# Which queue issues the stores and the first loads of a fused attention and adapter kernel

## The chip, the cores and the metric

The kernel runs on one core of one Trainium2 chip. The metric is the device time of one execution in microseconds (us); several executions are timed and their median is given. A core has a TensorE (PE) for matrix products, a VectorE (DVE), a ScalarE (ACT), a GpSimd (POOL) and a SyncE (SP), each working through its own list of instructions in order, and 16 DMA engines that move data between HBM and the on-chip memory. A transfer is started by an instruction of ACT, SP or POOL; the profile calls the transfers of SP queue q1, those of ACT queue q10 and those of POOL queue q0.

## What is computed

Two stages follow one another. The first is an attention over channels: for each of four batches, with 6400 tokens of 256 channels,

```
qn = q / (norm of q over the tokens + 1e-6)
kn = k / (norm of k over the tokens + 1e-6)
a  = softmax(kn^T @ qn / tau, last axis)       # 256 x 256
x  = v @ a                                     # 6400 x 256
```

The second is a mixture of eight adapters of rank 16 on each of the 25600 rows of x:

```
logits = x @ w_gate ; the two largest are kept, softmax over the two gives w
out = x + sum over the two: w * (x @ A[e]) @ B[e]
```

Inputs and output are float32: q, k and v of 26.2 MB each are read, and 26.2 MB are written.

## The kernel before

A batch's 6400 tokens lie as 128 partitions by 50 chunks of 256 channels, so that a partition reads and writes a contiguous piece of HBM. Two chunks make a pair (`NPAIR` = 25 in a batch, `NPT` = 100 in all). Pairs make groups of `GRP` = 5; the last batch has groups of 5, 5, 5, 5, 3 and 2 pairs, so the last three groups are the pairs 90 to 94, 95 to 97, and 98 and 99.

**Loads.** q, k and v are loaded by GpSimd (`load_more`, L129 to L154), and the transfer turns float32 into bfloat16 on its way. The list `loads` holds their order, and a load is issued when a buffer of its kind is free. The exceptions stand at L158 to L167: the first four chunks (`FIRST`) of q and k of batch 0 are loaded as float32 by SP into a tile `stage`, and cast by DVE and ACT (L177, L178). Behind them on SP come three small constant loads, `wst`, `bst` and `ast`. ACT's first instruction is a load of its function table (L79).

**Compute.** Batch 0 first runs its Gram matrix (`gram`) and norms (`norm`) alone, then a chain of small steps (`chain0` to `chain6`) makes the softmax. After that, a loop over slots works on one pair at a time: transposing v (`transposes`), gating (`logits`, `gating`), adapters (`z_gz`, `gz_t`), product with the attention (`y_mm`), and `delta`, which adds the adapters' part and copies the sum from PSUM into the group's float32 tile `ys` by ACT (L510). The Gram matrices of batches 1 to 3 are laid between these pairs, slot by slot, by the table `GRAM`. There are nine `ys` buffers (`YB`), the first of which holds `stage` at the start.

**Stores.** A finished group is put in the list `unsent`. `send(keep)` (L517) issues one transfer for each whole group (1280 KB) when more than `keep` groups are waiting. `keep` is 7 during most of the run, so that stores are held back behind loads, and falls to 0 over the last slots. While `keep` is positive, ACT issues the store (15 of the 18 whole groups); at 0, SP does (the last three). The pairs from 90 on (`u >= NPT - 2 * GRP`) are stored one by one by SP, right after their copy, ten transfers of 256 KB (L513).

**Landing counters.** Each transfer has a semaphore that counts its landing, once for each of the 16 DMA engines. The trace shows eight such semaphores for all transfers of SP and ACT together, used in turn: a transfer waits on its own queue until the eighth one before it has landed.

Of the kernel before, what the change touches and what calls it, by code (L numbers as in the profile page):

```python
# [8 lines left out]
FP32 = mybir.dt.float32  # L9
# [7 lines left out]
def kernel(  # L17
# [16 lines left out]
    nc = tc.nc  # L34
    B, N, C = q.shape
    P = 128
# [9 lines left out]
    NPAIR = NC // 2  # L46
    NPT = B * NPAIR
    GRP = 5
    QKB, VB, YB = 4, 3, 9
    VP = [18, 16, 16]  # L50
    FIRST = 4
# [5 lines left out]
    q_v = q.rearrange("b (p c) d -> b p c d", p=P)  # L57
    k_v = k.rearrange("b (p c) d -> b p c d", p=P)
    v_v = v.rearrange("b (p c) d -> b p c d", p=P)
    out_v = out.rearrange("(b p c) d -> b p c d", b=B, p=P)  # L60
# [6 lines left out]
    y_pool = ctx.enter_context(tc.tile_pool(name="yp", bufs=YB))  # L67
# [8 lines left out]
    ps_y = ctx.enter_context(tc.tile_pool(name="psy", bufs=2, space=bass.MemoryType.PSUM))  # L76

    ctx.enter_context(tc.manual_schedule())
    nc.scalar.preload_act_table_set("natural_log_exp_and_others")  # L79


# [2 lines left out]
    for b, (first, last) in GRAM.items():  # L84
        n = last - first + 1
# [30 lines left out]
    def piece(kind, c):  # L116

        if kind == "qk":
            return divmod(c, PC)
        s = 0  # L120
        while c >= VP[s]:
            c -= VP[s]
            s += 1
        return s, c

    def used(kind, b, c, n):
        left[kind][where[kind, b, piece(kind, c)[0]]] -= n
# [26 lines left out]
            limit -= 1  # L154

    room = y_pool.tile([P, 2 * GRP, C], FP32, tag="ys", name="stage")  # L158
    stage = room[:, 0:2 * FIRST, :].rearrange("p (w c) d -> p w c d", w=2)
    nc.sync.dma_start(stage[:, 0, :, :], q_v[0, :, 0:FIRST, :])  # L160
    nc.sync.dma_start(stage[:, 1, :, :], k_v[0, :, 0:FIRST, :])
    wst = const.tile([P, CC * E], FP32)
    ast = room[:, 2 * FIRST, :].rearrange("p (e r) -> p e r", e=E)
    bst = room[:, 2 * FIRST + 1, :]
# [183 lines left out]
    free_banks = [False]  # L348
    unsent = []

    def transposes(g, eng):

        b, p = divmod(g, NPAIR)
        gr = groups[g]
        if "vT" not in gr:
            gr["vT"] = vt_pool.tile([P, CC, 2 * GRP, P], BF16, tag="vT", name="vT")
        s, o = piece("v", 2 * p)
        vt = tiles["v"][b, s]
        full = ps_t.tile([P, 512], FP32, tag="pt", name="vT_ps")
        pt = full[:, 0:256].bitcast(BF16).rearrange("p (c t) -> p c t", c=CC)  # L360
        i = 0
        for sc in range(2):
            for ic in range(CC):
                nc.tensor.matmul(pt[:, ic, sc * P:(sc + 1) * P],  # L364
                                 vt[:, o + sc, ic * P:(ic + 1) * P], ident,
                                 is_transpose=True, start=(i == 0), stop=(i == 3))
                i += 1
        used("v", b, 2 * p, 2)
        w = 2 * (g - gr["f"])
        dst = gr["vT"][:, :, w:w + 2, :]  # L370
        src = pt.rearrange("p c (s t) -> p c s t", s=2)
        if eng == "act":
            nc.scalar.copy(dst, src)  # L373
        else:
            nc.vector.tensor_copy(dst, src)  # L375
        gr["full"] = full
        pr[g] = {"vT": dst, "w": w}
# [125 lines left out]
    def delta(u):  # L503
        r, gr = pr.pop(u), groups[u]
        for sc in range(2):
            nc.tensor.matmul(r["y"][:, sc, :], r["gzT"][:, sc, :], ball_sb, start=False,  # L506
                             stop=(sc == 1), skip_group_check=True)
        if "ys" not in gr:
            gr["ys"] = y_pool.tile([P, 2 * GRP, C], FP32, tag="ys", name="ys")
        nc.scalar.copy(gr["ys"][:, r["w"]:r["w"] + 2, :], r["y"])  # L510
        if u >= NPT - 2 * GRP:
            c0 = 2 * (u % NPAIR)
            nc.sync.dma_start(out_v[gr["b"], :, c0:c0 + 2, :], gr["ys"][:, r["w"]:r["w"] + 2, :])  # L513
        elif u == gr["f"] + gr["n"] - 1:
            unsent.append(gr)

    def send(keep):  # L517


        eng = nc.scalar if keep else nc.sync  # L520
        while len(unsent) > keep:
            gr = unsent.pop(0)
            c0, n = 2 * (gr["f"] - gr["b"] * NPAIR), 2 * gr["n"]
            eng.dma_start(out_v[gr["b"], :, c0:c0 + n, :], gr["ys"][:, 0:n, :])
# [43 lines left out]
    while nz < NPT or zq is not None or dq is not None:  # L568
# [12 lines left out]
        u = None  # L581
        if nz < min(slot, NPT) and groups[nz]["ready"]:
            u = nz
# [7 lines left out]
        if slot < NPT and not behind:  # L591
            transposes(slot, "dve" if items or f is chain3 else "act")
        if dq is not None:
            delta(dq)
        dq, zq = zq, u
        send(max(0, min(DEFER, DEFER - (slot - GRAM[B - 1][1]) // 4)))
        if behind:
            deal(0.3)
# [52 lines left out]
```

## Time and profile before

| | |
|---|---|
| median of 3 runs | 256.47 us (256.42 to 256.54) |
| profiled execution, its own time | 256.67 us |
| its span, first to last instruction | 254.9 us |
| busy share of the span | PE 86%, ACT 69%, DVE 60%, POOL 13% |
| HBM read and written | 78.91 MB and 26.21 MB, 412 GB/s over the span |
| stores by ACT, whole groups | 15 of 1280 KB, 13.7 us from issue to landing (median) |
| stores by SP, whole groups | 3 of 1280 KB, 10.8 us |
| stores by SP, single pairs | 10 of 256 KB, 5.9 us |

The span is shorter than the execution's own time by what lies around it. The profile's DMA rows count the bytes that a transfer writes; a load that turns float32 into bfloat16 reads twice what it writes, so 213 GB/s written in the loading stage stand for 426 GB/s read.

### The profile page before, as it was taken

What the parts mean: (1) busy time and instruction counts of PE and PEld (TensorE: products, weight loads), DVE (VectorE), ACT (ScalarE), POOL (GpSimd) and SP (SyncE); (2) the same over time, 40 slices, a digit from 0 to 9 for tenths busy, and PEclk for the clock granted to TensorE, in tenths of its full rate; (3) what the DMA queues carried; (4) which work ended last, traced back from release to release, by engine and by line L of the source; (5) the groups of instructions that cost most, each with busy time, mean ns of one, the idle gap of its engine ahead of it and who ended that gap; (6) DMA issues with size and microseconds to landing.
All of it is one profiled execution on the core that took longest, in us unless ns stands there. A gap on an engine that the chain in (4) does not pass through costs nothing.

```text
span 254.9 us, 7402 instructions
## 1 busy us (share of the span) xinstructions
PE 219.1 (86%) x3106; PEld 189.2 (74%) x3106; DVE 152.6 (60%) x577; ACT 176.3 (69%) x290; POOL 32.5 (13%) x67
## 2 busy tenths in 40 slices
PE   0787792986999999999999999989999899999950
PEld 0444460875998878989999779879997799999930
DVE  1322335463757769676686685747587876778720
ACT  2434344676687797877976978778866777887850
POOL 8031221121112102020111011000000200000000
PEclk9999998697999999999999999999999999999996
DMA  7999999999999999999999999999999999999986
GB/s 210 225 215 216 212 217 214 213 215 216 213 213 215 221 209 214 221 209 218 211 219 213 214 297 233 259 270 284 252 299 295 382 331 356 425 425 418 425 359 231
DMA packets 14177, 66.80 MB, mean 262 GB/s; under 512 B 2624, under 2 KB 2752, under 8 KB 10816
## 3 DMA queue, kind: packets, MB, share of 16 engines
q0 software_dynamic: 8496, 38.80, 74.6%
q10 hardware_dynamic: 2160, 19.66, 18.7%
q1 hardware_dynamic: 3488, 7.87, 8.5%
q8 instruction: 24, 0.39, 0.6%
q14 instruction: 9, 0.07, 0.1%
HBM read 78.91 MB, written 26.21 MB: 412 GB/s over the span
## 4 chain that ended last, share of the span: by engine, by line
DMA 43%; PE 43%; DVE 5%; ACT 2%; POOL 2%; issue 2%; DVEq 0%; ACTq 0%; POOLq 0%
DMA vt<-in_v_dram 21%; PE y_ps L486 11%; DMA qk<-in_k_dram 9%; DMA qk<-in_q_dram 8%; PE acc L217 7%; PE y_ps L506 5%; DMA out_dram<-ys 5%; PE zg L470 5%; PE vT_ps L364 5%; PE zg L494 3%; PE vT_ps L385 3%; PE nrm L234 2%; DVE gz L474 1%; PE nrm L228 1%; POOL qk L148 1%
## 5 line engine op out<-in xcount | busy, mean ns | idle before, releaser
L207 ACT ACTIVATE sq<-qk 128x1024 bf16<-128x1024 bf16 x87 | 89.6, 1054 | 22.7 <-DMA qk<-in_k_dram 17.4
L217 PE MATMUL acc<-qk 128*128 128x256 bf16 x400 | 74.1, 286 | 15.3 <-DMA qk<-in_k_dram 8.8
L510 ACT COPY ys<-y_ps 128x512 f32<-128x512 f32 x100 | 58.7, 587 | 22.8 <-PE y_ps L506 19.3
L486 PE MATMUL y_ps<-a_bf,vT 128*128 128x256 bf16 x400 | 59.9, 272 | 0.3 <-ACT ys L510 0.3
L217 PEld LDWEIGHTS <-qk 128*128 128x128 bf16 x400 | 34.3, 101 | 25.2 <-DMA qk<-in_k_dram 11.4
L474 DVE TENSOR_TENSOR gz<-zg,gate 128x256 bf16<-128x256 f32 x100 | 41.7, 418 | 14.4 <-PE zg L470 12.9
L375 DVE COPY vT<-vT_ps 128x512 bf16<-128x512 bf16 x63 | 26.7, 424 | 29.0 <-PE vT_ps L364 28.3
L364 PE MATMUL vT_ps<-ident,vt 128*128 128x128 bf16 x400 | 39.5, 222 | 2.2 <-DMA vt<-in_v_dram 1.9
L234 PEld LDWEIGHTS <-sq 128*128 128x128 bf16 x600 | 36.1, 98 | 7.0 <-ACT sq L207 3.0
L470 PE MATMUL zg<-wa_sb,vT 128*128 128x128 bf16 x400 | 38.5, 219 | 1.2 <-DVE gzT L500 1.0
L506 PE MATMUL y_ps<-ball_sb,gzT 128*128 128x256 bf16 x200 | 38.2, 273 | 0.0
L234 PE MATMUL nrm<-ones_bf,sq 128*128 128x1 bf16 x600 | 35.7, 165 | 1.2 <-ACT sq L207 1.2
L486 PEld LDWEIGHTS <-vT 128*128 128x128 bf16 x400 | 33.5, 97 | 3.1 <-issue 0.4
L364 PEld LDWEIGHTS <-vt 128*128 128x128 bf16 x400 | 30.0, 99 | 5.2 <-DMA vt<-in_v_dram 2.7
L373 ACT COPY vT<-vT_ps 128x512 bf16<-128x512 bf16 x37 | 21.7, 587 | 10.2 <-PE vT_ps L364 8.9
L494 PE MATMUL zg<-ident,gz 128*128 128x128 bf16 x200 | 27.7, 221 | 1.1 <-DVE gz L474 0.6
L470 PEld LDWEIGHTS <-vT 128*128 128x128 bf16 x400 | 26.0, 97 | 3.3 <-issue 2.2
L500 DVE COPY gzT<-zg 128x256 bf16<-128x256 bf16 x90 | 25.3, 281 | 0.0
L148 POOL DMA_DIRECT2D qk<-in_q_dram x21 | 11.5, 547 | 88.4 <-ACT sq L207 19.4
L209 DVE TENSOR_TENSOR sq<-qk 128x1024 bf16<-128x1024 bf16 x13 | 9.1, 697 | 22.2 <-DMA qk<-in_k_dram 14.2
L151 POOL DMA_DIRECT2D vt<-in_v_dram x17 | 9.0, 534 | 65.7 <-PE y_ps L506 49.2
L494 PEld LDWEIGHTS <-gz 128*128 128x128 bf16 x200 | 15.2, 98 | 2.9 <-DVE gz L474 2.5
(61 smaller groups left out, 182.6 us busy)
## 6 DMA issues: line engine op xcount, KB each, us to landing
out_dram<-ys ACTq DMA_DIRECT2D x15, 1280.0 KB, 13.7
qk<-in_q_dram POOLq DMA_DIRECT2D x18, 640.0 KB, 21.2
qk<-in_k_dram POOLq DMA_DIRECT2D x18, 640.0 KB, 23.4
vt<-in_v_dram POOLq DMA_DIRECT2D x5, 1024.0 KB, 28.4
out_dram<-ys SPq DMA_DIRECT2D x3, 1280.0 KB, 10.8
vt<-in_v_dram POOLq DMA_DIRECT2D x3, 1152.0 KB, 26.2
vt<-in_v_dram POOLq DMA_DIRECT2D x6, 512.0 KB, 22.2
out_dram<-ys SPq DMA_DIRECT2D x10, 256.0 KB, 5.9
```

The source lines that it names most:

```text
L207: nc.scalar.activation(sq, src, ACT.Square)
L217: nc.tensor.matmul(acc[b][:, ic, :], t[:, 1, o, ic * P:(ic + 1) * P], t[:, 0, o, :], start=(c == 0 and ic == 0), stop=(c == NC - 1), skip_ ...
L234: nc.tensor.matmul(nrm[b][:, j:j + 1], sq[:, w, c % 2, ic * P:(ic + 1) * P], ones_bf[:, 0:1], start=(c == 0 and j == 0), stop=(c == NC - 1 ...
L364: nc.tensor.matmul(pt[:, ic, sc * P:(sc + 1) * P], vt[:, o + sc, ic * P:(ic + 1) * P], ident, is_transpose=True, start=(i == 0), stop=(i = ...
L375: nc.vector.tensor_copy(dst, src)
L470: nc.tensor.matmul(z[:, sc, :], r["vT"][:, ic, sc, :], st[b]["wa"][:, ic, E:E + ER], start=(sc == 0 and ic == 0), stop=(sc == 1 and ic == ...
L474: nc.vector.tensor_tensor(out=gz.rearrange("p c (e r) -> p c e r", e=E), in0=z.rearrange("p c (e r) -> p c e r", e=E), in1=gr["gate"][:, r ...
L486: nc.tensor.matmul(y[:, sc, :], r["vT"][:, ic, sc, :], st[b]["a"][:, ic, :], start=(sc == 0 and ic == 0), stop=False, skip_group_check=True)
L494: nc.tensor.matmul(gt[:, sc, :], r["gz"][:, sc, :], ident, is_transpose=True, start=(sc == 0), stop=(sc == 1))
L500: nc.vector.tensor_copy(gzT, gt)
L506: nc.tensor.matmul(r["y"][:, sc, :], r["gzT"][:, sc, :], ball_sb, start=False, stop=(sc == 1), skip_group_check=True)
L510: nc.scalar.copy(gr["ys"][:, r["w"]:r["w"] + 2, :], r["y"])
```

## The change

Three things move. First, the float32 load of k's first chunks is issued by ACT, and stands ahead of ACT's table load; q's stays on SP, and `wst`, `bst` and `ast` follow directly behind it. Second, every whole group is stored by ACT, also the last three. Third, the pairs from 90 on are still stored by SP, but in seven transfers: after pairs 91, 93 and 96 two pairs together (512 KB), and after pairs 94, 97, 98 and 99 a single pair (256 KB).

```diff
@@ top of the kernel
     ctx.enter_context(tc.manual_schedule())
+
+    room = y_pool.tile([P, 2 * GRP, C], FP32, tag="ys", name="stage")
+    stage = room[:, 0:2 * FIRST, :].rearrange("p (w c) d -> p w c d", w=2)
+    nc.sync.dma_start(stage[:, 0, :, :], q_v[0, :, 0:FIRST, :])
+    nc.scalar.dma_start(stage[:, 1, :, :], k_v[0, :, 0:FIRST, :])
     nc.scalar.preload_act_table_set("natural_log_exp_and_others")
...
-    room = y_pool.tile([P, 2 * GRP, C], FP32, tag="ys", name="stage")
-    stage = room[:, 0:2 * FIRST, :].rearrange("p (w c) d -> p w c d", w=2)
-    nc.sync.dma_start(stage[:, 0, :, :], q_v[0, :, 0:FIRST, :])
-    nc.sync.dma_start(stage[:, 1, :, :], k_v[0, :, 0:FIRST, :])
     wst = const.tile([P, CC * E], FP32)
...
     unsent = []
+
+    LAST = {NPT - 9: 4, NPT - 7: 4, NPT - 6: 2, NPT - 4: 4, NPT - 3: 2, NPT - 2: 2, NPT - 1: 2}
...
         nc.scalar.copy(gr["ys"][:, r["w"]:r["w"] + 2, :], r["y"])
-        if u >= NPT - 2 * GRP:
-            c0 = 2 * (u % NPAIR)
-            nc.sync.dma_start(out_v[gr["b"], :, c0:c0 + 2, :], gr["ys"][:, r["w"]:r["w"] + 2, :])
+        if u in LAST:
+            n = LAST[u]
+            c0, w = 2 * (u % NPAIR) + 2 - n, r["w"] + 2 - n
+            nc.sync.dma_start(out_v[gr["b"], :, c0:c0 + n, :], gr["ys"][:, w:w + n, :])
+        elif u >= NPT - 2 * GRP:
+            pass
         elif u == gr["f"] + gr["n"] - 1:
             unsent.append(gr)
 
     def send(keep):
...
-        eng = nc.scalar if keep else nc.sync
+        eng = nc.scalar
         while len(unsent) > keep:
```

## The prediction

> **What bounds the kernel now.** I looked first at the page's DMA rows.
>
> ```profile
> DMA  7999999999999999999999999999999999999986
> GB/s 210 225 215 216 212 217 214 213 215 216 213 213 215 221 209 214 221 209 218 211 219 213 214 297 233 259 270 284 252 299 295 382 331 356 425 425 418 425 359 231
> q0 software_dynamic: 8496, 38.80, 74.6%
> q10 hardware_dynamic: 2160, 19.66, 18.7%
> q1 hardware_dynamic: 3488, 7.87, 8.5%
> ```
>
> The 16 DMA engines are full in every slice but the first and the last two. Loads alone write 213 GB/s and so read 426; stores alone run at 425. The kernel is bound by its transfers from end to end, and time can only be won or lost where an engine stands idle, or in what a packet costs. That leaves the start and the end. I then asked for windows there (columns: window, its length, busy time of PE, PEld, DVE, ACT and POOL, clock, DMA share, GB/s).
>
> ```profile
> 0.00:2.00 2.00, 0.00 (x0) 0.00 (x0) 0.32 (x3) 1.27 (x1) 0.97 (x6) 1.00 0.23 31
> 2.00:4.00 2.00, 0.00 (x0) 0.00 (x0) 0.00 (x0) 0.02 (x1) 2.00 (x5) 1.00 0.88 293
> ...
> 228.00:234.00 6.00, 5.89 (x101) 5.45 (x99) 4.14 (x21) 4.60 (x10) 0.00 (x0) 1.00 1.01 422
> 234.00:240.00 6.00, 6.00 (x82) 5.57 (x80) 4.78 (x22) 5.21 (x13) 0.00 (x0) 1.00 1.00 423
> 240.00:246.00 6.00, 5.37 (x56) 4.28 (x53) 2.82 (x13) 4.89 (x13) 0.00 (x0) 1.00 1.01 413
> 246.00:248.50 2.50, 0.00 (x0) 0.00 (x0) 0.00 (x0) 0.34 (x1) 0.00 (x0) 1.00 0.74 286
> 248.50:251.50 3.00, 0.00 (x0) 0.00 (x0) 0.00 (x0) 0.00 (x0) 0.00 (x0) 0.82 1.04 396
> 251.50:254.90 3.40, 0.00 (x0) 0.00 (x0) 0.00 (x0) 0.00 (x0) 0.00 (x0) 0.50 0.23 86
> ```
>
> Compute ends at 246.3, 7 us before the last store has landed. Between 246 and 248.5 the engines are a quarter idle: a hole of 0.26 x 2.5 = 0.65 us. SP's own rows tell why (the second is from the wait list of 246 to 255 us).
>
> ```profile
> 247.41 2.43 SPq L513 DMA_DIRECT2D out_dram<-ys  x5
> ...
> SPq L513 <- DMA out_dram<-ys: 3.5, 1, 3.5
> ```
>
> The sixth single-pair store waits on SP for a landing, and five stores go out together at 247.41. The landing is that of the store eight places earlier, which ACT issued at 223.36 and which took 24.0 us, because from 224 on SP's whole groups shared the engines with it.
>
> **Who is idle in the hole?** That decides the change. I read it from the landing records, sixteen for each store, one for each DMA engine. The first and last engine of the last five stores are at 249.26 and 250.97, 249.94 and 251.64, 250.64 and 252.28, 251.32 and 252.93, 252.01 and 253.56. In each, six engines are in a cluster at the front and ten trail by up to 1.6 us. The latest record of the ten stores steps by 0.64 us from the second on (247.76, 248.40, 249.04, 249.69, 250.33, 250.97, 251.64, 252.28, 252.93, 253.56) and takes no break at the hole: from 250.33 to 250.97, between a store issued before it and one issued after, it is also 0.64. So the engine that ends the kernel never ran dry; the hole lies on engines that were ahead. Every transfer is cut evenly over the 16, so no other engine takes over its share.
>
> **Start: k on ACT.** Removed: one issue on SP, so `wst`, `bst` and `ast` are issued 0.42 us earlier. Added: one issue on ACT, some 0.4 us by SP's row, ahead of a table load of 1.28 us. The table load then ends near 2.4; ACT's first real work is at 5.89, where it waited 3.88 us, so that is covered. The first packet comes at 1.74, 1.0 us after q's issue at 0.74. From there the engines are occupied, but the first packets are slow:
>
> ```profile
> DMA packets 65, 0.27 MB, mean 177 GB/s; under 512 B 0, under 2 KB 0, under 8 KB 65
> DMA packets 158, 0.58 MB, mean 388 GB/s; under 512 B 16, under 2 KB 16, under 8 KB 158
> ```
>
> These are the windows 1.5 to 3 and 3 to 4.5 us. The 65 packets take 307 ns on average, and the later ones of the same 4096 bytes 159 (median), so the slow beginning costs 65 x 148 ns / 16 = 0.6 us on each engine. No row shows two queues beginning together. If the second hides the first's slow packets, that is a gain of up to 0.6; if k's queue pays such a beginning of its own, a loss of 0.6, and of 1.1 on the slowest engine (first packet about 1.9, q landed at 4.56, eight packets of 159 ns are 1.27, landing some 0.3, as 253.56 stands to the last packet's end at 253.24). I take 0: the nearest row is k itself, which came second on these engines and showed no slow beginning (landed 1.31 us after q, eight packets of 159 ns). The slow beginning belongs to the engine's first packets, whichever queue they come from. Until GpSimd's first packets at 4.82 the small loads give the engines work in either order, and GpSimd's next issue that waits for compute, at 15.05, has eight loads queued until 28.7 before it. A later q costs nothing.
>
> The Trainium skill ("DMA: Bandwidth & Descriptors", section "Issuing engines are not separate DMA queues") says that transfers issued from several engines share the same 16 DMA engines and that only the sequencer's issue time is saved. By that rule, moving k is worth at most its issue time, 0.42 us, and moving the stores nothing. The 422 GB/s above, with two queues, against 425 with one agree on the second half.
>
> **End: whole groups on ACT.** Three issues leave SP for ACT, 0.34 us each. On ACT such an issue lies beside the running copy:
>
> ```profile
> 221.42 0.58 ACT L373 COPY vT<-vT_ps 128x512 bf16<-128x512 bf16 x1
> 221.65 0.34 ACTq L524 DMA_DIRECT2D out_dram<-ys  x1
> 221.91 0.59 ACT L510 COPY ys<-y_ps 128x512 f32<-128x512 f32 x1
> ```
>
> New is a wait: the groups ending with pairs 84 and 89 are issued right behind the copy that finishes them, so ACT's queue stands until that copy has ended. For pair 84 (copy ends at 229.34) ACT's next work waited for PE until 229.98: covered. For pair 89 (ends 236.05) the next `gzT` copy began at 235.99 and now comes after the issue, some 0.4 us later; PE and DVE wait behind it and compute ends near 246.7. The first of the three, pair 79, goes out near 229 instead of 222.52. None of this reaches the end while the queues are full: at 222.34 eight whole groups and the ten pairs had yet to land, 8 x 3.07 + 10 x 0.64 = 31.0 us for the slowest engine, hence 253.3 (seen: 253.56). The same bytes remain after the change.
>
> **End: seven pieces for ten.** By the eight counters, the last store waits for the group of pair 84, the one before it for pair 79's. On ACT's queue alone the groups land 3.07 us apart; from 225.9 that puts the group of pair 74 near 238 and, with SP's pieces in between, pair 79's at 241 to 244 and pair 84's at 245.5 to 249.5. A last issue at 247 to 249.5 still finds the last whole group, 3.07 us, ahead on the slowest engine. The hole goes, and the end does not notice. What it does notice is packets: three times, 16 packets of 2048 bytes at 84 ns and two counters (9 ns) become 8 of 4096 bytes at 159 and one, 1362 - 1281 = 81 ns; by the landing steps, 2 x 0.64 against a 4096-byte packet interpolated at 157 ns, 24 ns. So 0.07 to 0.24; I take 0.15.
>
> **Sum.** On the profiled execution: 256.67 - 0 - 0.15 = 256.52. Its own time lies 0.20 above the median, so the median becomes 256.3.
>
> **Rivals.**
> *The hole was on the path.* If what lags in the queue at 246 is made up by the others, its 0.65 us come back: 256.47 - 0.65 - 0.15 = 255.7, and with an overlapped beginning 255.1. For it: the DMA row falls to 0.74 just before the end. Against it: the steps of 0.64.
> *ACT's queue pays its own beginning.* k's packets on a fresh queue are slow like q's, and the slowest engine carries 1.1 us to the end: 256.47 + 1.1 - 0.15 = 257.4. It decides when over 0.66 us of it lands on the slowest engine. For it: ACT's first transfer before, issued at 144.70, moved its first packet only at 148.11, 3.4 us later; against it, that one stood behind GpSimd's packets, and k paid nothing.
> *The change does nothing on the path*: the pieces' saving falls on engines that are ahead; 256.5.
>
> **How the numbers follow.** Forecast 0.55, nothing 0.10, hole 0.22, own beginning 0.13. 0.2% is 0.51 us, about what a measurement of this kernel can tell from no change. Faster by that: the hole, and 0.04 of the forecast where part of the beginning is hidden, 0.26. Slower: the own beginning and 0.01 of a last piece that comes late, 0.14. The rest is 0.60. The range leaves half of each outer case out, 255.6 to 257.0.
>
> **What would show it.** Right: no wait of SP for a landing of over 1 us after 240; DMA share at 1.0 between 246 and 248.5; last landing 0.1 to 0.2 earlier; steps of the latest record equal to the packets' time. Wrong: the six early engines and the ten late ones end together, more than 0.5 us earlier; or packets of k over 300 ns, and GpSimd's first loads landing later than 7.75 and 10.02.

## The result and the profile after

| | before | after |
|---|---|---|
| median of 22 runs each | 256.44 us (256.32 to 256.73) | 256.03 us (255.85 to 256.32) |
| ratio to before | | 0.9983, 95% interval 0.9977 to 0.9989 |
| profiled execution, own time and span | 256.67, 254.89 us | 256.08, 254.30 us |
| last copy of ACT ends | 246.34 | 247.32 |
| last store has landed | 253.56 | 253.28 |
| from there to the end of the span | 1.33 us | 1.02 us |
| landing counters checked behind the last landing | 8 | 3 |

The change is worth 0.44 us by the ratio (0.28 to 0.59), 0.17%: faster, but within the 0.2% that the prediction called no change. The forecast was 0.15 us.

The DMA rows of the page of after, to be laid beside those of before:

```profile
DMA  7999999999999999999999999999999999999996
GB/s 212 222 217 216 210 215 215 215 214 214 215 214 217 217 214 212 219 213 213 214 221 210 213 263 267 231 301 267 266 295 288 394 312 361 394 424 421 430 413 241
q10 hardware_dynamic: 2736, 24.12, 23.1%
q1 hardware_dynamic: 2480, 3.42, 4.1%
```

The last slice but one was 8 tenths busy before and is 9 or more now. 4.46 MB moved from SP's queue (q1) to ACT's (q10), and the two have 432 packets fewer together (5216 for 5648). The windows of after at both ends (columns as before):

```profile
2.00:4.00 2.00, 0.00 (x0) 0.00 (x0) 0.00 (x0) 0.46 (x1) 2.00 (x5) 1.00 0.87 293
...
240.00:246.00 6.00, 5.66 (x64) 4.81 (x62) 3.65 (x16) 4.91 (x13) 0.00 (x0) 1.00 1.00 415
246.00:248.50 2.50, 0.69 (x7) 0.38 (x4) 0.00 (x0) 1.17 (x2) 0.00 (x0) 1.00 0.99 403
248.50:251.50 3.00, 0.00 (x0) 0.00 (x0) 0.00 (x0) 0.00 (x0) 0.00 (x0) 0.59 0.89 352
251.50:254.30 2.80, 0.00 (x0) 0.00 (x0) 0.00 (x0) 0.00 (x0) 0.00 (x0) 0.50 0.24 91
```

The start is as it was: 293 GB/s between 2 and 4 us in both. The hole between 246 and 248.5 is closed, 0.99 in place of 0.74. But the idle time has only moved to the window behind it, where the share fell from 1.04 to 0.89. The engines that were ahead had waited in the middle; now they finish early. In the landing records of the last store, six engines are done by 251.12 and ten between 251.90 and 253.28.

SP's wait list of after, from 236 us on (what waits <- what it waits for: us in total, times, longest):

```profile
SPq L517 <- ACT gzT L501: 17.7, 4, 14.1
SPq L652 <- DMA out_dram<-ys: 5.1, 6, 1.5
SPq L517 <- ACT ys L513: 2.5, 3, 1.5
```

No store (L517) waits for a landing any more. L652, the launch, stands for what SP does at the very end: it checks the eight landing counters one by one, in a fixed order. In after six of these checks had to wait, each for a later landing. In before it was one:

```profile
SPq L646 <- DMA out_dram<-ys: 3.6, 1, 3.6
```

One wait of 3.6 us means that the counter checked first was the one that filled last. The trace's records give the times: the last landing of before at 253.56, then the eight checks at 253.574, 253.636, 253.700, 253.761, 253.821, 253.882, 253.941 and 254.003, some 61 ns apart, and the closing barrier of all engines behind them. I call the time from the last landing to the end of the span the close. After has 30 transfers of SP and ACT in place of 33; the last one is on the sixth counter, and three checks follow its landing.

### The profile page after: what moved, and what is told of

Its sections match the earlier page's. It is cut to its first block, busy times and chain, and to the rows that moved or that the text cites. A ratio compares the mean times of both kernels' runs of the same rounds, so it can differ in the third digit from the quotient of the medians.

```text
span 254.3 us, 7393 instructions
## 1 busy us (share of the span) xinstructions
PE 220.2 (87%) x3106; PEld 190.4 (75%) x3106; DVE 152.8 (60%) x577; ACT 176.1 (69%) x290; POOL 33.2 (13%) x67
## 4 chain that ended last, share of the span: by engine, by line
PE 57%; DMA 25%; DVE 7%; ACT 3%; issue 3%; POOL 1%; DVEq 0%; ACTq 0%; POOLq 0%
PE y_ps L489 15%; DMA qk<-in_k_dram 11%; PE acc L218 10%; DMA vt<-in_v_dram 9%; PE zg L473 7%; PE y_ps L509 7%; PE vT_ps L367 6%; DMA out_dram<-ys 5%; PE zg L497 4%; PE nrm L235 3%; PE vT_ps L388 3%; ACT sq L208 2%; DVE gz L477 2%; ACT ys L513 1%; DVE lm L423 1%
```

## The experiments

My theory after the comparison: the time lies in three places. The landing of the slowest DMA engine, which feels the packets and not the hole; the number of checks behind the last landing, which is the number of transfers counted in eights; and nothing in the start. The rivals: the hole was on the path after all, or the start gave the part that the packets do not explain. "Before" in each comparison is the kernel before on the same chip.

### Each part of the change by itself

Only k's load:

```diff
+    nc.scalar.dma_start(stage[:, 1, :, :], k_v[0, :, 0:FIRST, :])   # with q's, ahead of the table load
     nc.scalar.preload_act_table_set("natural_log_exp_and_others")
...
-    nc.sync.dma_start(stage[:, 1, :, :], k_v[0, :, 0:FIRST, :])
```

> Only k's first load moves to ACT; all stores as before. My theory (end of the kernel set by its latest DMA engine, and by the list of landings that SP walks through at the close; the start worth nothing): 0.0 +- 0.1 us against before, 256.44, q landing later (5.6 in place of 4.56) and GpSimd's second load still near 10.0. Rival 'start': the part of the measured gain that the packets do not explain, some 0.25 us, comes from here, so 256.2, with GpSimd's second load landing 0.2 to 0.3 earlier than 10.02.

Measured: 256.54 against 256.55 us, ratio 1.0002 (0.9993 to 1.0011). q landed at 5.52 in place of 4.56, GpSimd's first two loads at 7.96 and 9.88 in place of 7.75 and 10.02. The packet rows for 1.5 to 3 us and 3 to 4.5 us:

```profile
DMA packets 52, 0.21 MB, mean 142 GB/s; under 512 B 0, under 2 KB 0, under 8 KB 52
DMA packets 144, 0.59 MB, mean 393 GB/s; under 512 B 0, under 2 KB 0, under 8 KB 144
```

Two queues move no more in the first microseconds than one did (65 and 158 packets). Nor is the slow beginning paid twice: by the packet records, k's 128 packets on ACT's new queue took 176 ns on average, where q's took 234. The time shows nothing of either; an effect between -0.18 and +0.28 us stays possible.

Only the whole groups:

```diff
-        eng = nc.scalar if keep else nc.sync
+        eng = nc.scalar
```

> Only the three last whole groups move to ACT; ten single-pair stores as before, 33 transfers of SP and ACT in all as before. My theory: SP's long wait for a landing and the hole at 246 to 248.5 go, and the time stays, 0.0 to -0.1 us, because the hole lay on engines that were ahead. Rival 'hole on the path': the 0.65 us of the hole come back at least in part, -0.3 to -0.65 us.

Measured: 256.59 against 256.55 us, ratio 1.0001 (0.9993 to 1.0010). Its window 246 to 248.5 and SP's waits from 246 on:

```profile
246.00:248.50 2.50, 0.00 (x0) 0.00 (x0) 0.00 (x0) 0.39 (x1) 0.00 (x0) 1.00 0.86 339
...
SPq L646 <- DMA out_dram<-ys: 3.7, 1, 3.7
SPq L513 <- DMA out_dram<-ys: 3.1, 1, 3.1
```

The expectation that SP's long wait goes was a miss: the eighth piece now waits 3.1 us for the last whole group. The hole still half closed, from 0.74 to 0.86, that is 0.3 us more of work done in it, and the last landing stayed at 253.55. What is done early on the engines that are ahead does not reach the end.

Only the seven pieces (the `LAST` part of the diff, with `send` as before):

> Only the ten single-pair stores become seven; whole groups and k's load as before. My theory: packets -0.1 us (three times 0.03 to 0.08), and the close -0.3 us: with 30 transfers in place of 33 the last one uses the sixth of the eight landing counters and not the first, so SP has three checks of 61 ns behind the last landing and not eight; together -0.4 us, the whole measured gain. Rival 'hole': the piece after pair 98 now waits for the late store of pair 74's group, the hole stays in part, and no more than the packets' 0.1 us is gained.

Measured: 256.06 against 256.55 us, ratio 0.9981 (0.9972 to 0.9990); close 1.02 us, three checks. This part alone carries the whole gain. The wait that the rival names was there (2.3 us, for pair 98), but the hole was not (the window, and SP's waits from 236 us on):

```profile
246.00:248.50 2.50, 0.14 (x2) 0.00 (x0) 0.00 (x0) 0.69 (x2) 0.00 (x0) 1.00 1.00 405
...
SPq L517 <- DMA out_dram<-ys: 2.3, 1, 2.3
```

So this run doesn't separate the hole from the close; the next ones do.

### The close by itself

The kernel before, and the 8 KB load of the gate's weights in eight parts, so that 40 transfers are counted and not 33:

```diff
-    nc.sync.dma_start(wst, moe_w_gate.rearrange("(p cc) e -> p (cc e)", p=P))
+    w_v = moe_w_gate.rearrange("(p cc) e -> p (cc e)", p=P)
+    cuts = list(range(0, 129, 16))
+    nc.sync.dma_start(wst[0:cuts[1], :], w_v[0:cuts[1], :])
     ...
+    for i, j in zip(cuts[1:], cuts[2:]):          # behind bst and ast
+        nc.sync.dma_start(wst[i:j, :], w_v[i:j, :])
```

> The kernel before, but the 8 KB load of the gate's weights is cut into eight small loads on SP (seven of them behind the two other constants). Nothing else changes: q, k, the whole groups and the ten pieces go out as before. 40 transfers of SP and ACT in place of 33, so the last store uses the eighth landing counter in place of the first. Theory of the closing walk: seven checks of 61 ns fewer behind the last landing, -0.43 us, span minus last landing 0.9 in place of 1.33 us, and the last landing where it was, near 253.6. Rivals (hole, start, packets): 0.0 us, or a little slower for seven more small transfers.

Measured: 256.08 against 256.55 us, ratio 0.9985 (0.9976 to 0.9994). The window 246 to 248.5 and SP's waits from 246 on:

```profile
246.00:248.50 2.50, 0.00 (x0) 0.00 (x0) 0.00 (x0) 0.11 (x1) 0.00 (x0) 1.00 0.76 296
...
SPq L517 <- DMA out_dram<-ys: 3.7, 1, 3.7
SPq L650 <- DMA out_dram<-ys: 3.2, 6, 0.6
```

Hole and wait are nearly as in before (0.76 and 3.7 us, there 0.74 and 3.5), the ten pieces too. Only the last row differs: six short waits in place of one long one, and 0.91 us from the last landing to the end, 0.42 less, with one check behind it. A kernel that changes nothing but the count of its transfers is as fast as the changed kernel. Its last landing was at 253.26, 0.3 earlier than expected; this profiled run lay 0.14 us under its median and that of before 0.12 over the median of its partners here, which covers most of it.

The reverse, the changed kernel with that load in four parts (`cuts = list(range(0, 129, 32))`), 33 transfers:

> The changed kernel, but the load of the gate's weights is cut into four small loads. 33 transfers of SP and ACT in place of 30, so the last store uses the first landing counter again and all eight checks follow its landing. Theory of the closing walk: five checks of 61 ns come back, +0.3 us over the changed kernel, 256.35, close to the kernel before. Rivals (hole, start, packets): the changed kernel's 256.03.

Measured: 256.42 against 256.54 us, ratio 0.9992 (0.9984 to 1.0001); last landing 253.54, close 1.33 us.

```profile
246.00:248.50 2.50, 0.06 (x1) 0.00 (x0) 0.00 (x0) 0.61 (x2) 0.00 (x0) 1.00 1.00 409
...
SPq L656 <- DMA out_dram<-ys: 6.1, 1, 6.1
```

The row with one wait is back, and with it the eight checks; the hole is closed, and much of the gain is gone: by the ratio 0.2 us is left, between 0.41 and none (-0.03). The time alone would not settle it, since this interval overlaps that of the changed kernel (0.9977 to 0.9989); the close, read in the trace of each run, does for its part. With the run before, 0.3 of the 0.44 us follow the count of transfers and not the hole; the rest is looked at below.

### How much slack the end of compute has

The last pair's copy five times over:

```diff
-        nc.scalar.copy(gr["ys"][:, r["w"]:r["w"] + 2, :], r["y"])
+        for _ in range(5 if u == NPT - 1 else 1):
+            nc.scalar.copy(gr["ys"][:, r["w"]:r["w"] + 2, :], r["y"])
```

> The changed kernel, but the last pair's copy into the store's buffer is done five times over (4 x 0.59 = 2.4 us more), so that compute ends and the last store is issued 2.4 us later, near 249.7. My theory (the latest engine has work queued until 253, so the end of compute has slack): 0.0 +- 0.1 us against the changed kernel. Rival (compute's end or the last issue sets the time): +2.4 us.

Measured: 256.12 against 256.54 us, ratio 0.9983 (0.9974 to 0.9992), that of the changed kernel. The last store was issued 3.1 us after the one before it (0.65 in after) and landed at 253.39. Its issue was at 248.21 and not near 249.7, since compute was earlier in this execution (the store before it went out at 245.08, in after at 246.69).

With `range(11 ...)`:

> The same with eleven copies, 10 x 0.59 = 5.9 us more; the last store is issued near 253.2, when everything else has landed. My theory: now it does count; first packet 1 to 2 us later, 0.6 us of packets, landing 0.3, so the last landing near 255.5 to 256.2 in place of 253.3, +2.2 to +2.9 us. Rival (the end of compute is on the path): +5.9 us.

Measured: 257.21 us, ratio 1.0037 (1.0020 to 1.0054), +1.2 us over the changed kernel by the medians, less than expected. The seven runs lie in two bunches, five at 257.0 to 257.3 and two at 258.4 and 258.5; the profiled one is of the second, with its last copy ending at 253.57 and the last landing at 255.62. The issues from 253 to 254 us in it (size, us to landing):

```profile
out_dram<-ys SPq DMA_DIRECT2D x1, 256.0 KB, 2.0
```

This lone store of 256 KB took 2.02 us from issue to landing. So, by estimate, the last issue decides from 253.28 - 2.02 = 251.3 us on, 3.9 us later than after makes it. The fit in the Trainium skill ("DMA: Bandwidth & Descriptors", section "Anatomy of one DMA — SWDGE (gpsimd) path"), 2.0 us and the bytes at 436 GB/s, made for GpSimd's transfers, would give an estimate of 2.6 for it; the measured 2.02 stands. Compute's end differs between executions (246.1 to 247.3 in the profiles here); that this makes the two bunches is likely, since such a difference now counts, but the faster ones have no trace.

### The pieces by themselves

Before, with three whole stores for the last three groups and the weights' load in eight parts, which makes 33 transfers again:

```diff
-        if u >= NPT - 2 * GRP:
-            c0 = 2 * (u % NPAIR)
-            nc.sync.dma_start(out_v[gr["b"], :, c0:c0 + 2, :], gr["ys"][:, r["w"]:r["w"] + 2, :])
+        LAST = {NPT - 6: 10, NPT - 3: 6, NPT - 1: 4}
+        if u in LAST:                              # as in the change
```

> The kernel before, but its ten single-pair stores become three (1280, 768 and 512 KB, by SP, as the groups end), and the load of the gate's weights is cut into eight, so that SP and ACT issue 33 transfers as before and the last store is on the first landing counter again: eight checks follow it, the close stays at 1.33 us. What is left is the price of the packets: on the latest engine 20 chunks in packets of 10240, 6144 and 4096 bytes cost 6.14 us, in packets of 2048 bytes 6.40, so -0.26 us. Rival (the pieces cost nothing on the path, the whole gain of the change is the close): 0.0.

Measured: 256.18 against 256.59 us, ratio 0.9983 (0.9974 to 0.9992), -0.44 us (-0.21 to -0.67); close 1.34 us, last landing 252.94. The window 246 to 248.5 and SP's waits from 236 us on:

```profile
246.00:248.50 2.50, 0.00 (x0) 0.00 (x0) 0.00 (x0) 0.11 (x1) 0.00 (x0) 1.00 0.99 418
...
SPq L654 <- DMA out_dram<-ys: 6.4, 1, 6.4
```

So the three stores gain time with the close as in before. The -0.26 expected lies inside the interval, and so does the -0.56 of the packets' own times: 8 x (385 + 234 + 159) + 3 x 9 = 6251 ns for the three stores, 10 x (8 x 84 + 9) = 6810 for the ten. The hole closed here too, but the latest landing record shows the packets at work: its last two steps are 1.84 us for 768 KB and 1.24 for 512 KB, where before pays 3 x 0.64 and 2 x 0.64. How much more than the 0.26 the larger packets are worth, this run doesn't show.

The opposite, twenty stores of one chunk, 49 transfers:

> The opposite: each of the last twenty chunks is a store of its own (128 KB, packets of 1024 bytes), and the load of the gate's weights is cut into seven, which makes 49 transfers and again the first landing counter and eight checks. Price of the packets: 42 ns for one of 1024 bytes by the line through 2048 (80 ns) and 10240 bytes (384 ns), twenty times eight and a counter of 9 ns make 6.9 us, +0.5 us against before; by 57 ns, as such packets took in the load of B, 9.3 us, +2.9. Rival (the pieces cost nothing on the path): 0.0.

Measured: 258.86 against 256.59 us, ratio 1.0086 (1.0072 to 1.0100), +2.2 us. It doesn't show the price of small packets (46 ns for 1024 bytes), for another bound took over:

```profile
SPq L518 <- DMA out_dram<-ys: 5.9, 2, 4.3
...
246.00:248.50 2.50, 0.00 (x0) 0.00 (x0) 0.00 (x0) 0.51 (x1) 0.00 (x0) 1.00 0.61 212
```

SP stands until 247.21 for a landing, with fifteen stores left, and then issues one every 0.48 us until 254.0. The latest landing record steps by 0.48 too, and all 16 engines land within some 0.2 us of each other, so they wait for SP. In the kernel before, five stores were left at that point, at 0.47 us each against 0.64 of transfer, and the slowest engine still had work: the same wait was free.

### Three whole stores and one check

The changed kernel, with three whole stores for the last groups and the weights' load in seven parts, 32 transfers:

```diff
-    LAST = {NPT - 9: 4, NPT - 7: 4, NPT - 6: 2, NPT - 4: 4, NPT - 3: 2, NPT - 2: 2, NPT - 1: 2}
+    LAST = {NPT - 6: 10, NPT - 3: 6, NPT - 1: 4}
...
+    cuts = [0, 32, 48, 64, 80, 96, 112, 128]
```

> The changed kernel with the last three groups stored whole by SP (1280, 768 and 512 KB: three stores for seven), and the load of the gate's weights in seven parts, which makes 32 transfers of SP and ACT and puts the last store on the eighth landing counter. My theory: packets of 10240, 6144 and 4096 bytes for 20 chunks cost 6.14 us on the latest engine where the seven pieces cost 6.31, -0.17 us; two checks of 61 ns fewer at the close, -0.12; together -0.3 us against the changed kernel, 255.75. Rival (the last bytes must be spread finely so that the queues never run dry): slower than the changed kernel by up to 1 us.

Measured: 255.86 against 256.54 us, ratio 0.9969 (0.9957 to 0.9981), -0.80 us against before (-0.49 to -1.10). Its SP rows from 236 and from 246 us on:

```profile
241.51 5.48 SPq L521 DMA_DIRECT2D out_dram<-ys  x3
...
SPq L656 <- DMA out_dram<-ys: 5.4, 4, 1.8
```

Close 0.91 us, one check; last landing 252.88. Against the changed kernel the ratios say -0.36 us (0.9969 and 0.9983), where -0.3 was expected. Their intervals overlap a little, so that it is faster than before is shown, and that it beats the changed kernel is likely.

## Why the prediction was right or wrong

**What bounds the kernel: right.** The end is the landing of the slowest engine. The hole closed from 0.74 to 0.99 with the change, and `groups_on_act` and `after_four_w` closed it in part or wholly for 0.0 and 0.2 us, with last landings of 253.55 and 253.54 against 253.56. The rival that put 0.65 us there is out. The records of before show whose hole it was: from the fifth single-pair store to the sixth, the first engine's landing goes from 246.63 to 249.26, 2.63 us in place of 0.64, and the latest one's by 0.64 as always. Some six engines that led by up to 3.7 us lost 2.0 of it; 6 x 2.0 of 16 x 2.5 us is 0.30, about the share that the hole lacks (0.26). One reading was a little off: behind the hole the lead is 1.71 us and not 1.6 at the first of the five stores, by the prediction's own times, and seven engines land within 0.3 us of the first there, not six.

**Start: right.** 0 was taken between -0.6 and +1.1; `k_on_act` measured +0.05 us (-0.18 to +0.28). The rule of shared engines in the Trainium skill ("DMA: Bandwidth & Descriptors", section "Issuing engines are not separate DMA queues") agrees with this run (ratio 1.0002) and with `groups_on_act` (1.0001), and the issue time of 0.42 us that it allows did not reach the end. ACT's queue moved its first packet at 2.14, 0.4 us after SP's, though both were issued at 0.74. The prediction took the engines as occupied from the first packet on. By the packet records they were busy 0.69 of the time between 1.74 and 2.14 us in before and 0.59 in after, and 0.99 and 0.89 from there to 3 us. This loss, too, did not reach the end.

**Whole groups on ACT: right in sum.** Predicted were a wait of ACT behind the copies of pairs 84 and 89, and compute ending 0.4 us later:

```profile
229.73 0.59 ACT L513 COPY ys<-y_ps 128x512 f32<-128x512 f32 x1
230.35 0.64 ACTq L530 DMA_DIRECT2D out_dram<-ys  x1
```

The wait is there (the issue starts as the copy ends), the issue took 0.64 us and not 0.34 for pair 84, and the last copy ended 1.0 us later than before. But that is not the wait's doing, and here the prediction's step failed: the issue at 221.65 in before stands at 222.63 in after, so compute was already 1.0 us later ahead of the first store that changes its queue, and with the groups alone moved (`groups_on_act`) the last copy ended at 246.39 against 246.34, with the issue ahead of it 0.06 later too (221.71 against 221.65). No run shows the 0.4 us at the end of compute. Nor would they count, with 3.9 us of slack. The groups of pairs 79 and 84 landed at 240.8 and 244.1, earlier than the 241 to 244 and 245.5 to 249.5 of the prediction, which had SP's pieces in between; in after SP's first piece moved no packet before 242.63.

**Seven pieces: right, as far as the noise lets one see.** 0.07 to 0.24 was the range, 0.15 the value. The changed kernel with eight checks is 0.2 us below before (0.41 below to 0.03 above). The three-store run, at 0.44 for 0.26 to 0.56, fits either end of the range.

**The sum: a term was missing.** It went from the last landing straight to the time, as if what follows were constant. The 1.33 us behind it hold eight checks of 61 ns when the last store is on the first counter, and the change, with three transfers fewer, takes five of them away: 0.31 us. The sum should have read 0.31 + 0.07 to 0.24, that is 0.38 to 0.55; 0.44 was measured. The prediction used the eight counters to see which store waits for which, and had SP's wait list to 255 us at hand, in which the close is one wait; it did not ask in which order they are checked at the end. That is why the forecast was a third of the gain. The time lay in the range because the range was wide, made for the rivals, and not because the sum was right.

**What would show it.** No wait of SP for a landing, a share near 1.0 in the hole, and steps equal to the packets' time (512 KB pieces 1.18 and 1.25 us, 256 KB 0.62 to 0.64) came as written. The last landing was to move by 0.1 to 0.2 and moved by 0.28 in the profiled pair, whose own times lie 0.59 apart where the medians lie 0.41. Of the signs of being wrong, GpSimd's first load did land later (8.12 for 7.75, the second at 10.01 for 10.02), but k's packets took 181 ns on average in after and not over 300, so the rival of ACT's own beginning is out.

## What to carry to other kernels

When transfers bind a kernel to its end, a hole in the mean DMA share need not be worth time; here it was free, because the engine that lands last did not stand idle in it. Read the latest landing record of consecutive transfers: here its steps went on unbroken at 0.64 us. Make the last stores large, as long as enough is queued that the engines do not see them come late, and mind the issuing queue's own pace when there are many. And count what stands behind the last landing: here the number of transfers, taken in eights, moved the end by up to 0.42 us, as much as anything done to the data.

## What the runs showed of the hardware that was not expected

- The close of the program depends on which landing counter the last transfer uses: 1.33 us with eight checks behind it, 1.02 with three, 0.91 with one.
- The 16 DMA engines do not finish a transfer together: at the last store the first one is 1.6 us ahead of the slowest in before and 2.8 in after, and six or seven land in a cluster at the front. Why was not settled.
- ACT's issue of a whole group took 0.34 us (median of before, 0.43 at most), but 0.64 us for pair 84's in after (0.35 to 0.76 in the other five runs that make this move), with four of its whole groups not yet landed. The issue at 224.34 in after had as many before it and took 0.34, so the full queue alone doesn't explain it; that stays open.
